# Four layers forward and backward on one core: the last chunks' pieces by a table of their own, a turned weight by TensorE, and another order of the weight gradients

## The chip, the cores and the metric

The kernel runs on one core of a Trainium2 chip, as a single launch. The metric is the device time of that launch in microseconds (us). Engines are named as in the profile: PE is TensorE, DVE is VectorE, ACT is ScalarE, POOL is GpSimd, and SP is the engine whose queue issues the DMAs here.

## The reference

Four residual layers, A, B, A, B, over an input x of 2048 rows and 640 columns (bfloat16); each normalises x, projects to q, k, v (a weight of 640 x 1920), attends with 32 heads of 20 columns, and projects back (640 x 640). A and B use the same weights in both of their layers. What is returned is the output and the gradients for x and for the four weights.

```python
def A(x):            # linear attention
    q, k, v = heads(layernorm(x) @ wqkv_A)
    phi = lambda t: where(t > 0, t + 1, exp(t)) + 1e-6
    pq, pk = phi(q), phi(k)
    kv, z = einsum("bhsd,bhse->bhde", pk, v), einsum("bhsd->bhd", pk)
    num, den = einsum("bhqd,bhde->bhqe", pq, kv), einsum("bhqd,bhd->bhq", pq, z)[..., None] + 1e-6
    return merge(num / den) @ wo_A
def B(x):            # softmax attention over the 256 rows before
    q, k, v = heads(layernorm(x) @ wqkv_B)
    s = where(mask, einsum("bhqd,bhkd->bhqk", q, k) * Dh ** -0.5, -1e9)
    return merge(softmax(s) @ v) @ wo_B
x = x + A(x); x = x + B(x); x = x + A(x); x = x + B(x)
# returned: x, and the gradients of x, wqkv_A, wo_A, wqkv_B, wo_B for a given grad_out
```

## The kernel before

Rows are taken in 16 tiles of 128, and in the backward of B in NC = 8 chunks of two tiles. The layers are numbered 0 (A), 1 (B), 2 (A), 3 (B).

Nearly all of the order is written by hand. A *plan* is a list of (place, function); `slots` sorts it into slots, and a loop runs the functions of each slot, each of which issues a few instructions. So each engine's order is that of the plan. A DMA is issued by SP, in the order in which a scheduler puts the loads and stores; the queue is served in order, so a DMA that waits for its source or its buffer holds up those behind it. Places come from the table `PLACES`.

The stages in order of time:

- **Forward** (to some 650 us). `forward` goes through layers 0 to 3, and a layer's tiles are interleaved with the next's. B1 = 138 is the slot where layer 1 begins its scores. In layer 0 a tile is projected (`dense<-WA,h2T`), mapped by phi (`plan_feat`, pq and pk on DVE) and stored. Beside that the weight of A is turned for later use: `turn(k)` issues 15 transposing DMAs (`tw<-in_A_wqkv_dram`), two every 12 slots from slot 41.6, `keep_turned` stores them, four at a time, to `WTAt` in DRAM; the linear backwards load them back as `WTA`. The turned rows lie in ring buffers of the attention, which `home` gives back.
- **Backward of layer 3** (some 660 to 1099.7). `core` runs the attention backward over the 8 chunks: scores, exponentials, dp, ds, flips of ds, and accumulations (`acc`). In the slots of chunk c there also stand the pieces *behind* an earlier chunk, by `plan_behind` from the table's list `bh`: turn dq (`turn`), dh = dq times the turned weight (`dense<-WTB,dqT`, 30 products a tile), layer norm backward (`ln`, `ln2`: DVE, ACT, POOL's dh and gn), flip gn, multiply by Wo (`dense<-WoTA,gT`, 10 a tile), and from that the linear layer's dn (`prod`, `fold`, `red`), whose outer products with pq (`outer<-dn,pqb`) sum up to dmz. The pieces behind chunk c stand 32 slots after those of c+1's start; for the last chunk 16 earlier than that. What has no slot left in `core` is returned as `left3`.
- **Drain of layer 3** (1099.7 to 1151.7). `left3` runs, with nothing between its pieces but the loads of the next stage; behind its end `close_outer` and `turn_outer` form dmz and dmzT.
- **Linear backward of layer 2** (to some 1263). `plan_linear` for 16 tiles, 8 slots apart: load dn, v, pqk, hn, g, flip them, multiply with mz, dmz, dmzT, then dqkv, dh by `WTA`, layer norm backward. Its first tile begins 3 slots before the drain's end. At its end the first chunk of the next attention backward is prepared (`plan_before`, places `n1`).
- **Backward of layer 1** (to 1692.93) and its **drain** (`left1`, to some 1770), as for layer 3. Between the pieces of this drain stand the first products of the weight gradients.
- **Linear backward of layer 0** (to 1996.8), with weight gradients between: `fill(0.8)` issues 0.8 us of them in each slot.
- **The rest of the weight gradients** (to 2160).

`weight_jobs` yields the weight gradients one product at a time (`wg<-rhs,lhs`). A matrix is made in blocks of 240 or 320 columns (480 for two layers' sum once `W.wide` is set). For each block it loads the right operand (`rhs`), for each matrix the left (`lhs`: hn or o of a layer); in mode `all` both layers are summed, in mode `add` one layer is summed in PSUM and the other's part, made early (`early_weights`, `wgp`) and kept in DRAM, is loaded (`part`) and added. The order of the matrices is

```python
mats = [mat("all", "B", "W", (3, 1)), mat("add", "B", "Wo", (1,)), mat("all", "A", "W", (2, 0)), mat("add", "A", "Wo", (0,))]
```

Of the kernel before, what the change touches and what calls it, by code (L numbers as in the profile page):

```python
# [33 lines left out]
CW = D // 2  # L34
LN_EPS = 1e-5
# [20 lines left out]
class Kern:  # L56
# [183 lines left out]
    def forward(self, st):  # L240
# [59 lines left out]
        def turn(k):  # L300
            i, j = divmod(k, 4)
            if j == 0:
                turned[i] = rings[i].tile([P, 4, D], BF, name=f"tw{i}", tag="T")
            self.dma(turned[i][:, j, :], self.W["A"][:, k * P:(k + 1) * P], transpose=True, behind=True)
# [7 lines left out]
        plan += [(41.6 + 6 * (k // 2), lambda k=k: turn(k)) for k in range(NF)] + [(57.5 + 12 * i, lambda i=i: keep_turned(i)) for i in range(4)] + [(96 + i, lambda i=i: home(i)) for i in range(5)]  # L312
# [605 lines left out]
    def plan_behind(self, st, l, c, dq, g_out):  # L918
# [44 lines left out]
        late = l == 1 and c >= TT // 2 - 2  # L963
        plan = [(0 if ex else 13 if last else A[26], load), (-6 if last else A[27], lambda: turn(0)), (-5 if last else A[28], lambda: turn(1)),
                ((-2 if l == 1 else 14) if last else 26 if l == 3 and c == TT // 2 - 2 else A[29], store), (0 if ex else 13 if late else A[30], load_o), (A[9] + 3, store_g),
                (1 if ex else 14 if late else A[31], load_q), (A[23] + 6, store_dn), (A[24], outer, .54, 0, 378), (A[25], outer, .54, 0, 378)]
        for i in range(2):
            a = A[12 * i:12 * i + 12]
# [649 lines left out]
```

## Time and profile before

| | |
|---|---|
| median of 3 runs | 2164.93 us (2164.41 to 2165.44) |
| the profiled execution | 2161.81 us, its span 2160.1 |
| granted TensorE clock, mean | 0.973 |
| PE busy | 1990.3 us, 92% |
| DVE busy | 1350.9 us, 63% |
| ACT busy | 1362.2 us, 63% |
| POOL busy | 1040.5 us, 48% |
| DMA | 433.48 MB in 729096 packets, 201 GB/s |

The profile is of one execution. Busy times are shares of its span; times in the trace count from the span's start. In a row of the timeline stand the start, the length, the engine, the line, the operation, out<-in by the program's names, shape and type, how many instructions were put together, and in brackets the idle time before and what ended it. A row of several matmuls that follow each other is longer than what they cost, since the last one's way through the array counts: the cost is the distance to the next row's start. In the slices, each digit is a fortieth of the span (54 us) and tells tenths.

### The profile page before, as it was taken

To read this page: it belongs to the slowest core of one execution; us is meant where nothing else is said; L and a number is where in the kernel's file an instruction comes from. 1 tells how busy PE (TensorE), PEld (TensorE's weight loads), DVE (VectorE), ACT (ScalarE), POOL (GpSimd) and SP (SyncE) were. 2 spreads that over 40 slices of the span, in tenths; PEclk is the share of its full clock that TensorE was granted. 3 is DMA by queue.
4 is the path that set the end of the run, shared out by engine and by line. 5 is a ranking of instruction groups with operands and counts; after the bars stand their busy time and mean duration, and the time that the engine had idled before them with its cause. 6 is when DMAs were issued, how large, how long until landed. Compare 5 with 4: busy or idle time off the path is not lost. (4 is left out here: it accounts for less than half of the span.)

```text
span 2160.1 us, 76461 instructions
## 1 busy us (share of the span) xinstructions
PE 1990.3 (92%) x32383; PEld 1547.6 (72%) x32383; DVE 1350.9 (63%) x2765; ACT 1362.2 (63%) x1897; POOL 1040.5 (48%) x1663
## 2 busy tenths in 40 slices
PE   7899998799988999999988989989999889999999
PEld 5567776577766877777767868777777678887546
DVE  6788886878754677777746856777777423333001
ACT  5458888378876788888845767888888414332000
POOL 2046666156666457777643455577776401222000
PEclk9999999999998999999998999999999999999999
DMA  9798897589886779999988962799988987999843
GB/s 275 213 222 218 216 216 170 137 213 220 211 212 189 141 161 189 189 191 180 181 238 266 261 193 75 157 189 189 195 179 182 255 271 229 258 223 249 265 120 93
DMA packets 729096, 433.48 MB, mean 201 GB/s; under 512 B 447024, under 2 KB 711344, under 8 KB 728496
## 3 DMA queue, kind: packets, MB, share of 16 engines
q1 hardware_dynamic: 728752, 428.59, 81.2%
q8 instruction: 253, 4.15, 0.8%
q14 instruction: 91, 0.75, 0.1%
HBM read 194.35 MB, written 144.70 MB: 157 GB/s over the span
## 5 line engine op out<-in xcount | busy, mean ns | idle before, releaser
L763 DVE TENSOR_TENSOR ds<-dp,e 128x1024 bf16<-128x1024 f32 (+1 forms) x384 | 443.7, 1155 | 162.6 <-PE s L146 73.3
L759 ACT ACTIVATE e<-s 128x1024 bf16<-128x1024 f32 (+1 forms) x384 | 378.3, 985 | 89.7 <-PE s L146 84.5
L399 ACT ACTIVATE eT<-sT 128x2048 bf16<-128x2048 f32 x180 | 338.0, 1878 | 96.1 <-PE sT L146 84.8
L146 PE MATMUL wg<-rhs,lhs 128*128 128x240 bf16 (+2 forms) x2400 | 334.0, 294 | 9.7 <-DMA lhs<-hn 9.7
L146 PEld LDWEIGHTS <-lhs 128*128 128x128 bf16 x2400 | 232.6, 99 | 86.1 <-DMA lhs<-hn 12.0
L778 POOL TENSOR_SCALAR_AFFINE_SELECT e<-e 128x256 bf16<-128x256 bf16 x512 | 201.6, 409 | 181.8 <-ACT e L759 150.8
L146 PEld LDWEIGHTS <-dqT 128*128 128x128 bf16 x1920 | 169.8, 98 | 65.8 <-issue 8.7
L407 POOL TENSOR_SCALAR_AFFINE_SELECT eT<-eT 128x512 bf16<-128x512 bf16 x256 | 165.0, 648 | 101.4 <-ACT eT L399 101.4
L792 ACT COPY dsT<-flip 128x1024 bf16<-128x1024 bf16 (+1 forms) x200 | 191.2, 956 | 21.9 <-PE flip L787 20.1
L146 PE MATMUL acc<-slabqs,ds 128*128 128x20 bf16 x2880 | 194.6, 172 | 1.7 <-ACT dq L847 1.0
L146 PE MATMUL acc<-ds,e 128*128 128x20 bf16 x2880 | 192.7, 171 | 0.1
L146 PE MATMUL dp<-slabT,dT 32*128 32x128 bf16 (+1 forms) x1952 | 152.1, 245 | 39.2 <-DVE ds L763 33.7
L146 PEld LDWEIGHTS <-ds 128*128 128x128 bf16 x2880 | 176.2, 96 | 10.6 <-issue 6.6
L774 POOL TENSOR_SCALAR_AFFINE_SELECT e<-e 128x512 bf16<-128x512 bf16 x224 | 142.9, 638 | 62.0 <-ACT e L759 59.0
L146 PEld LDWEIGHTS <-e 128*128 128x128 bf16 x2880 | 164.1, 96 | 7.8 <-issue 2.2
L1148 POOL TENSOR_TENSOR dh<-dh,lg 128x640 f32<-128x640 f32 x32 | 46.0, 1438 | 249.6 <-DVE s L1145 241.4
L146 PE MATMUL dense<-WB,hnT 128*128 128x320 bf16 x960 | 161.3, 302 | 0.5 <-DVE s L522 0.3
L146 PE MATMUL dense<-WTA,dqT 128*128 128x320 bf16 x960 | 161.4, 299 | 0.3 <-DVE dqT L1122 0.3
L146 PE MATMUL dense<-WTB,dqT 128*128 128x320 bf16 x960 | 156.3, 302 | 1.9 <-DMA dqT<-dq 1.9
L146 PE MATMUL s<-slabT,slabqT 32*128 32x128 bf16 (+1 forms) x1952 | 147.6, 245 | 6.6 <-ACT e L759 5.6
L410 POOL TENSOR_SCALAR_AFFINE_SELECT eT<-eT 128x512 bf16<-128x512 bf16 x224 | 143.3, 640 | 18.3 <-ACT eT L399 17.1
L787 PE MATMUL flip<-ident,ds 128*128 128x128 bf16 x1824 | 146.9, 222 | 4.2 <-DVE ds L884 4.0
(180 smaller groups left out, 4220.8 us busy)
## 6 DMA issues: line engine op xcount, KB each, us to landing
T<-T SPq DMA_DIRECT2D x96, 256.0 KB, 3.2
rhs<-dqkv SPq DMA_DIRECT2D x40, 480.0 KB, 5.1
s<-s SPq DMA_DIRECT2D x32, 512.0 KB, 3.8
slabT<-T SPq DMA_DIRECT2D x64, 256.0 KB, 4.0
dqkv<-dq SPq DMA_DIRECT2D x16, 960.0 KB, 5.8
dqkv<-dqa SPq DMA_DIRECT2D x32, 480.0 KB, 4.5
rhs<-dqkv SPq DMA_DIRECT2D x12, 960.0 KB, 7.6
hn<-hn SPq DMA_DIRECT2D x64, 160.0 KB, 2.8
```

Source lines behind the costliest of these rows:

```text
L146: return self.nc.tensor.matmul(out, lhsT=lhsT, rhs=rhs, start=start, stop=stop, skip_group_check=True, **kw)
L399: nc.scalar.activation(e, s, ACT.Exp)
L407: nc.gpsimd.affine_select(out=e, in_=e, compare_op=ALU.is_ge, fill=0.0, base=0, pattern=[[0, 4], [1, P]], channel_multiplier=-1)
L410: nc.gpsimd.affine_select(out=e, in_=e, compare_op=ALU.is_ge, fill=0.0, base=-1, pattern=[[0, 4], [-1, P]], channel_multiplier=1)
L759: nc.scalar.activation(u.e[:, :, 0:w], s[:, :, 0:w], ACT.Exp)
L763: nc.vector.tensor_tensor(out=d.ds[:, :, 0:w], in0=d.dp[:, :, 0:w], in1=d.e[:, :, 0:w], op=ALU.mult)
L774: nc.gpsimd.affine_select(out=v, in_=v, pattern=[[0, 4], [1 if far else -1, P]], **kw)
L778: nc.gpsimd.affine_select(out=v, in_=v, pattern=[[0, 2], [1 if far else -1, P]], **kw)
L787: nc.tensor.transpose(ps[:, 4 * j + i, :], f.ds[:, j, i * P:(i + 1) * P], self.ident)
L792: nc.scalar.copy(v(f.dsT), v(ps))
L1148: nc.gpsimd.tensor_tensor(out=x["dh"], in0=x["dh"], in1=L["g"][:, i, :], op=ALU.add)
```

## The change

It has these parts.

- In the forward, `turn(k)` no longer issues a transposing DMA: five flips on TensorE turn the 640 x 128 block k of A's weight, which is in the SBUF already, and ACT copies the result from PSUM. They stand at slots T0 + T1 k = 108 + 1.5 k; the stores (`keep_turned`) and `home` move behind them.
- The pieces behind the last two chunks of both attention backwards stand by a table of their own, `DRAIN`, counted from slot 32 NC + 7. The last chunk's loads go to buffers of the attention (`gb`, `ob`) and of the tag `dqT`, which has three. The PSUM pool of the drain opens before the first eleven left-over slots (before: behind the first eight). The linear tiles of layer 2 begin at slot 17 of the drain, that is inside it; dmz is closed at 21.2.
- The last tile of layer 2's linear backward has its `ln2` put into the second slot of the next attention; two pools of that attention (pd, pt) are opened at its third visit, since the linear stage's pools close that late. One preparing flip goes from place 9 to 23.
- `weight_jobs`: it starts at the first slot of layer 1's drain, and fills from the sixth; A's W comes ahead of B's Wo; parts are loaded up to 3 (8 at the end) ahead; 8 output buffers in the drain; `FILL` is 0.65 for 0.8; the buffers for the left operands open at other times (the third at slot 48 of the linear stage). `WTA` of layer 0 is loaded behind the first linear tile's loads. In all, 1280 products of 240 columns and 640 of 480 stand for 1600 and 480.

The diff, cut:

```diff
+T0, T1 = 108, 1.5
+DRAIN = {
+    -2: {"load": -3.4, "turn": (0.8, 0.9), "store": (1.3, 6), "o": 0.5, "q": 6, "g": 12, "dn": 16, "outer": (16.2, 16.7),
+         0: [1, 1.1, 1.2, 2, 2.1, 2.2, 2.5, 3.6, 5.6, 7.0, 7.1, 9.5],
+         1: [3.1, 3.2, 3.3, 4, 4.1, 4.2, 4.5, 5.5, 8.5, 9.2, 9.3, 12]},
+    -1: {"load": -2, "turn": (2.9, 3), "store": (3.9, 10), "o": 6.6, "q": 4.6, "g": 16, "dn": 22, "outer": (20.1, 20.5),
+         0: [5, 5.1, 5.2, 6, 6.1, 6.2, 6.5, 8.6, 11, 12.2, 12.3, 16],
+         1: [8, 8.1, 8.2, 9, 9.1, 9.15, 9.45, 10.6, 13, 14.2, 14.3, 20]}}
+FILL = 0.65
...
+        if name == "dqT":
+            bufs = 3
...
-                turned[i] = rings[i].tile([P, 4, D], BF, name=f"tw{i}", tag="T")
-            self.dma(turned[i][:, j, :], self.W["A"][:, k * P:(k + 1) * P], transpose=True, behind=True)
+                turned[i] = rings[4 - i].tile([P, 4, D], BF, name=f"tw{i}", tag="T")
+            tp = st.ps.tile([P, 8, P], BF, name="flip", tag="m")
+            for a in range(DT):
+                nc.tensor.transpose(tp[:, a, :], WA[:, a, k * P:(k + 1) * P], self.ident)
+            nc.scalar.copy(turned[i][:, j, :], tp[:, 0:DT, :].rearrange("p a b -> p (a b)"))
...
-        plan += [(41.6 + 6 * (k // 2), lambda k=k: turn(k)) for k in range(NF)] + [(57.5 + 12 * i, lambda i=i: keep_turned(i)) for i in range(4)] + [(96 + i, lambda i=i: home(i)) for i in range(5)]
+        plan += [(T0 + T1 * k, lambda k=k: turn(k)) for k in range(NF)] + [(T0 + T1 * min(4 * i + 4, NF) + 1, lambda i=i: keep_turned(i)) for i in range(4)]
+        plan += [((B1 - 32 if i == 0 else T0 + T1 * NF + 2), lambda i=i: home(i)) for i in range(5)]
...
-        ex = last and l == 1
-            x["hn"] = self.load(st.ex if ex else st.sp, "hnb", self.pair(self.hn[l], c), [P, 2, D])
-            x["g"] = self.load(st.ex if ex else st.sp, "gc", self.pair(self.gs[l], c), [P, 2, D])
+            x["hn"] = self.load(*((B.sp, "gb") if last else (st.sp, "hnb")), self.pair(self.hn[l], c), [P, 2, D])
+            x["g"] = self.load(*((B.sp, "ob") if last else (st.sp, "gc")), self.pair(self.gs[l], c), [P, 2, D])
...
-            x["o"] = self.load(st.ex if ex else st.sp, "oa", self.pair(self.o[la], c), [P, 2, D])
+            x["o"] = self.load(st.sp, "oa" if not last else "dqT", self.pair(self.o[la], c), [P, 2, D])
...
-            x["pq"] = self.load(st.ex if ex else st.sp, "pqb", self.pair(self.sv[la]["pqk"], c)[:, :, 0:D], [P, 2, D])
+            x["pq"] = self.load(st.sp, "pqb" if not last else "dqT", self.pair(self.sv[la]["pqk"], c)[:, :, 0:D], [P, 2, D])
...
-            a = A[12 * i:12 * i + 12]
+            a = A[12 * i:12 * i + 12] if D0 is None else D0[i]
...
-            plan += [(32 * (c + 2) - (16 if c == NC - 1 else 0) + a, *f)
-                     for a, *f in self.plan_behind(st, l, c, dq, g_out)]
+            at = 32 * NC + 7 if c >= NC - 2 else 32 * (c + 2)
+            plan += [(at + a, *f) for a, *f in self.plan_behind(st, l, c, dq, g_out, B)]
...
+                        if n == 3 and B.late is not None:
+                            B.late()
+                            self.core_buffers2(st, B)
...
-        mats = [mat("all", "B", "W", (3, 1)), mat("add", "B", "Wo", (1,)), mat("all", "A", "W", (2, 0)), mat("add", "A", "Wo", (0,))]
+        mats = [mat("all", "B", "W", (3, 1)), mat("all", "A", "W", (2, 0)), mat("add", "B", "Wo", (1,)), mat("add", "A", "Wo", (0,))]
...
-                if m["mode"] == "add" or nxt[1] is not None and nxt[1]["mode"] == "add" and j > 2:
+                while len(pt) < W.ahead and (m["mode"] == "add" or nxt[1] is not None and nxt[1]["mode"] == "add" and j > 1):
...
-            base = len(left3) - 3
+            base = 17 - 11
...
+                one = self.plan_linear(st, lp, 2, t, X, WTA, self.gs[1])
+                if t == TT - 1:
+                    ln2 = one.pop(-3)[1]
...
-            hooks = self.slots([(a - 20, f) for a, f, *_ in fs if a >= 20], 8)
+            hooks = self.slots([(2, ln2)] + [(a - 20, f) for a, f, *_ in fs if a >= 20], 8)
...
-                if j == 8:
+                if j == 0:
                     next(jobs)
-                if j == 20:
-                    self.dma(WTA.rearrange("p a b -> p (a b)"), self.WTA)
-                if j > 24:
+                if j > 4:
                     fill(1.0)
...
-                    fill(0.8)
-            W.lhs += [wl, wl3]
+                    if n == 8:
+                        self.after(self.dma(WTA.rearrange("p a b -> p (a b)"), self.WTA), lp.loaded)
+                    if n == 48:
+                        W.lhs += [wl3]
+                    fill(FILL)
+            wl4 = self.pool(rest, "wl", 1)
+            W.lhs += [wl4, wl, wl]
```

More of the change, by code (lines that the diff above doesn't have):

```diff
@@ L962, in plan_behind @@
         A = PLACES["bh"]
[L963 to L966, printed above, removed]
+        D0 = DRAIN.get(c - TT // 2)
+        if D0 is not None:
+            plan = [(D0["load"], load), (D0["turn"][0], lambda: turn(0)), (D0["turn"][1], lambda: turn(1)), (D0["store"][l // 2], store), (D0["o"], load_o),
+                    (D0["g"], store_g), (D0["q"], load_q), (D0["dn"], store_dn), (D0["outer"][0], outer), (D0["outer"][1], outer)]
+        else:
+            plan = [(A[26], load), (A[27], lambda: turn(0)), (A[28], lambda: turn(1)), (A[29], store), (A[30], load_o), (A[9] + 3, store_g),
+                    (A[31], load_q), (A[23] + 6, store_dn), (A[24], outer), (A[25], outer)]
         for i in range(2):
-            a = A[12 * i:12 * i + 12]
+            a = A[12 * i:12 * i + 12] if D0 is None else D0[i]
             t = 2 * c + i
@@ L1209, in part @@
         def part(m, c0, j, w):
-            t = W.out.tile([P, 320], F32, name="pt", bufs=3)
+            t = W.pts.tile([P, 320], F32, name="pt", bufs=W.ahead)
             self.dma(t, m["part"][:, j * D + c0:j * D + c0 + w])
@@ L1473, in passes @@
             for t in range(TT):
-                plan += [(max(base + 8 * t + a, 0), f) for a, f in self.plan_linear(st, lp, 2, t, X, WTA, self.gs[1])]
+                one = self.plan_linear(st, lp, 2, t, X, WTA, self.gs[1])
+                if t == TT - 1:
+                    ln2 = one.pop(-3)[1]
+                plan += [(max(base + 8 * t + a, 0), f) for a, f in one]
             def begin():
@@ L1533, in passes @@
             self.turn_outer(st, self.dmz, self.dmzT)
+            W.out = out
             psl.close()
@@ L1548, in passes @@
                     plan += [(8 * t + a + 14, f) for a, f in self.plan_linear(st, lp, 0, t, X, WTA, self.out_gx)]
-                for f in self.slots(plan, int(max(a for a, *_ in plan)) + 1):
+                for n, f in enumerate(self.slots(plan, int(max(a for a, *_ in plan)) + 1)):
                     if f is not None:
                         f()
-                    fill(0.8)
-            W.lhs += [wl, wl3]
+                    if n == 8:
[5 more added lines that the diff above has]
+            W.lhs += [wl4, wl, wl]
             W.wide, W.wq2 = True, self.pool(rest, "wq2", 1)
-            W.out, W.most = self.pool(rest, "wo2", 4), 480
+            W.out, W.most, W.ahead = self.pool(rest, "wo2", 4), 480, 8
+            W.pts = W.out
             fill(1e9)
```

47 lines of the change are left out of this document (26 added, 21 removed).

## The prediction

> **What bounds the kernel now.** I read the page's head and engine shares first, then its slices, then busy time by stretch, and last the timeline of TensorE in each stretch where it is idle.
>
> ```profile
> span 2160.1 us, 76461 instructions
> PE 1990.3 (92%) x32383; PEld 1547.6 (72%) x32383; DVE 1350.9 (63%) x2765; ACT 1362.2 (63%) x1897; POOL 1040.5 (48%) x1663
> ...
> PE   7899998799988999999988989989999889999999
> ...
> PEclk9999999999998999999998999999999999999999
> ```
>
> TensorE is busy for 92% of the span: the kernel is bound by it, and what can be won by moving work is the 169.8 us in which it is idle, and the places where its clock is below 1. Of the places that the digits show, the change touches the start (7, 8), the 21st and 22nd slice (from 1080) and the 32nd and 33rd (from 1674); a share over a slice hides a short wait, so the rows by stretch give their size (columns: length, busy time of PE, PEld, DVE, ACT, POOL with counts, then granted clock, DMA share, GB/s):
>
> ```profile
> 95.00:121.48 26.48, 20.28 (x158) 13.88 (x157) 20.64 (x57) 3.78 (x7) 1.10 (x2) 0.81 0.39 113
> 1099.70:1151.66 51.96, 37.95 (x298) 27.41 (x295) 17.85 (x42) 16.90 (x33) 20.09 (x16) 0.83 0.87 286
> 1200.00:1240.00 40.00, 39.97 (x480) 32.96 (x478) 34.10 (x68) 29.82 (x61) 17.87 (x13) 1.00 1.02 264
> 1692.93:1776.00 83.07, 69.79 (x614) 57.47 (x611) 19.27 (x45) 17.30 (x36) 20.11 (x16) 0.91 0.97 300
> 1840.00:1880.00 40.00, 40.00 (x428) 35.66 (x426) 13.66 (x34) 13.56 (x28) 8.27 (x6) 1.00 1.03 250
> 1996.80:2010.00 13.20, 6.89 (x34) 4.60 (x34) 0.41 (x1) 0.00 (x0) 0.00 (x0) 0.65 1.04 341
> ```
>
> The two drains (the left-over pieces behind the attention backward of layer 3, from 1099.70, and of layer 1, from 1692.93) leave TensorE idle for 14.0 and 13.3 us; behind the last linear tile, at 1996.8, 6.3 of 13.2 us are idle at clock 0.65. Inside the linear backwards (1200 to 1240, 1840 to 1880) nothing is idle. The change touches all of these places; the attention backwards themselves keep their order, so I cost the places one by one and take the rest as it is.
>
> **Part 1, forward: A's W turned by TensorE.** The forward's first layer, in its steady state, has a period that the flips of hn show:
>
> ```profile
> 49.13 0.44 PE L163 MATMUL flip<-ident,hn 128*128 128x128 bf16 x5
> ...
> 53.82 0.44 PE L163 MATMUL flip<-ident,hn 128*128 128x128 bf16 x5
> ...
> 58.73 2.83 PE L146 MATMUL dense<-WA,h2T 128*128 128x320 bf16 x10 [3.78 <-DVE pk L602]
> ...
> 64.01 0.44 PE L163 MATMUL flip<-ident,hn 128*128 128x128 bf16 x5
> ...
> 78.48 0.44 PE L163 MATMUL flip<-ident,hn 128*128 128x128 bf16 x5
> ...
> 84.87 0.33 PE L163 MATMUL flip<-ident,hn 128*128 128x128 bf16 x3
> ```
>
> ```profile
> 58.18 0.49 DVE L602 SCALAR_TENSOR_TENSOR pk<-dense,e 128x320 bf16<-128x320 f32 x1 [4.13 <-DMA pqk<-pk]
> ```
>
> ```profile
> 49.19 3.51 SPq L110 DMA_TRANSPOSE tw<-in_A_wqkv_dram  x2
> ...
> 53.43 0.38 SPq L110 DMA_DIRECT2D pqk<-pk  x1
> ```
>
> The period is 53.82 - 49.13 = 4.69 us, so 53.82 to 64.01 loses 10.19 - 4.69 = 5.5 and 78.48 to 84.87 loses 6.39 - 4.69 = 1.7: 7.2 us. TensorE waits for DVE's pk, DVE for the store of an earlier pk to leave its buffer, and that store sits in SP's queue behind two transposes that hold the queue for 3.51. The change takes all 15 transposes out of that queue, and I see nothing else there that comes late: 7.2 goes. In their place stand 15 groups of five flips on TensorE. Five take 49.41 - 49.13, about 0.28 us of the engine (the next dense starts there), 4.2 in all. Some six fall into its busy stretch and cost 6 x 0.28 = 1.7. The other nine fall behind 95 us, where it has 26.48 - 20.28 = 6.2 idle, waiting for DVE, at clock 0.81: at most 9 x 0.28 / 0.81 = 3.1, and I take half, 1.5. The 15 copies of 128x640 go to ACT, busy for 3.78 of 26.48 there, so nothing. Gain 7.2 - 3.2 = **4.0** (0.5, if half the stall has another cause and the rest is paid in full, to 7.2, if the flips cost nothing).
>
> The row shows a clock of 0.81 in that stretch, and I credit the flips with nothing for it. [...]
>
> **Part 2, drain of layer 3.** TensorE and POOL:
>
> ```profile
> 1105.83 8.31 PE L146 MATMUL dense<-WTB,dqT 128*128 128x320 bf16 x60
> 1115.35 0.45 PE L163 MATMUL flip<-ident,gn 128*128 128x128 bf16 x5 [1.21 <-POOL gn L1009]
> 1117.93 1.52 PE L146 MATMUL dense<-WoTA,gT 128*128 128x320 bf16 x5 [2.13 <-ACT gT L166]
> ...
> 1123.64 0.84 PE L146 MATMUL dense<-WoTA,gT 128*128 128x320 bf16 x5
> ...
> 1131.45 0.84 PE L146 MATMUL dense<-WTB,dqT 128*128 128x320 bf16 x5
> ...
> 1144.96 0.86 PE L146 MATMUL outer<-dn,pqb 128*120 128x126 bf16 x6 [3.84 <-DVE dn L1034]
> ...
> 1149.78 1.03 PE L210 MATMUL flip<-ident,dmz 120*126 120x120 bf16 x6 [1.11 <-DVE dmz L203]
> ...
> 1151.66 0.69 PE L146 MATMUL dense<-dmzT,vT 126*128 126x120 bf16 x7 [0.58 <-ACT dmzT L211]
> ```
>
> ```profile
> 1111.66 1.40 POOL L1002 TENSOR_TENSOR dh<-dh,gc 128x640 f32<-128x640 f32 x1 [15.40 <-DVE s L999]
> 1113.76 1.53 POOL L1009 TENSOR_TENSOR gn<-dh,lna 128x640 bf16<-128x640 f32 x1 [0.69 <-POOL dh L1002]
> ```
>
> The last of the 120 WTB products (dh of the last tile) ends at 1131.45 + 0.84 = 1132.29, 32.6 us into the drain; from there one chain (layer norm on DVE, dh and gn on POOL, flip, gT, WoTA, dn, outer, dmz turned) ends 19.4 later at 1151.66, where the first linear tile goes on. The new table puts ahead of that last product only the 45 flips of dq, the 120 WTB, 10 WoTA, 10 flips of gn and 12 outers: 130 x 8.31 / 60 = 18.0, 67 x 0.28 / 5 = 3.8, one wait for a copy, together 22. The chain behind it is the same 19.4, so 41.5 for 51.96: 10.4. I take **10** (6 to 14). Upwards: the first linear tile's flips and loads now stand inside the chain's idle time. Downwards: POOL now does four dh and four gn, with the products' folds among them, and if the last gn comes behind one more dh, gn and fold (1.40 + 1.53 + about as much), 4 are lost. Two loads of the last chunk now take buffers of the tag "dqT", so SP waits for a product to release one, and behind it wait the stores of dq and the first linear tile's loads; since three such buffers turn over every 15 products (2 us), I put that inside the 4.
>
> **Part 3, the join of the linear backward of layer 2 to the attention of layer 1.**
>
> ```profile
> 1272.81 0.69 DVE L763 TENSOR_TENSOR ds<-dp,e 128x512 bf16<-128x512 f32 x1 [8.19 <-DMA g<-lgn]
> ```
>
> ```profile
> 1268.60 1.54 POOL L1155 TENSOR_TENSOR lgn<-dh,lna 128x640 bf16<-128x640 f32 x1
> ```
>
> ```profile
> 1265.54 0.99 ACT L913 COPY dT<-flip 128x1024 bf16<-128x1024 bf16 x1
> ```
>
> DVE stands still for 8.19 here, and the attention's first pieces wait with it. The last tile's lgn (POOL, until 1270.14) stands ahead of the masks of the first scores, and a turn of dT (ACT, 0.99) ahead of their exponentials. The change puts the first two slots into the attention, the other 14 places later, and it opens two pools of the attention (pd, pt) only after three slots. I take **2.5**, the 1.54 and the 0.99; 0 if the pools opened late give the wait back, 4 at most, about half the 8.19.
>
> **Part 4, drain of layer 1, with weight gradients between.**
>
> ```profile
> 1731.31 0.78 PE L146 MATMUL wg<-rhs,lhs 128*128 128x240 bf16 x3 [1.09 <-DMA lhs<-hn]
> ...
> 1750.15 4.26 PE L146 MATMUL wg<-rhs,lhs 128*128 128x240 bf16 x40
> ...
> 1770.90 0.90 PE L163 MATMUL flip<-ident,ldn 128*126 128x128 bf16 x6 [4.37 <-DMA ldn<-dn]
> ```
>
> ```profile
> 1758.90 2.64 SPq L110 DMA_DIRECT2D lhs<-o  x4
> ```
>
> Idle are 13.3, shared among waits of some 1 us for the weight products' lhs (as at 1731.31) and those of the chain; 4.37 of it is the first linear tile's load behind four loads for Wo's products in SP's queue (2.64); Wo comes third now, so these are gone from there. The weight jobs load at the drain's first step and not at its ninth, and fill from its sixth. Of the idle time I leave 8: 5 in the chain before the first weight products have their operands, 2 at ldn, and 1 since WTA is loaded behind that tile. Gain 13.3 - 8 = 5.3, I take **5** (0 to 8); the clock's loss, 69.79 x 0.09 = 6.3, I leave as it is.
>
> **Part 5, linear backward of layer 0, and its end.**
>
> ```profile
> 2001.26 0.98 PE L146 MATMUL wg<-rhs,lhs 128*128 128x240 bf16 x4 [4.43 <-DMA lhs<-hn]
> ```
>
> Behind the last linear tile TensorE waits for the operands of A's W: 6.31 idle and 6.89 x 0.35 = 2.4 for the clock. With fill 0.65 some 200 products of B's W are left at that point, 200 x 4.26 / 40 = 21 us, under which A's operands come in (the new buffer opens there; four loads with 2.64 of issue land well inside 21). Gain **8.7** (4.5 if the last of them lands late, to 9). In the stage itself:
>
> ```profile
> 1225.78 0.51 PE L163 MATMUL flip<-ident,ldn 128*126 128x128 bf16 x6
> 1232.36 0.51 PE L163 MATMUL flip<-ident,ldn 128*126 128x128 bf16 x6
> ```
>
> A linear tile alone takes 6.58 at DMA share 1.02, which is 6.7 us of DMA. Between its parts stand now 51 weight products a tile (5.3 us, 12 in all), at 1.03, so 12.3 of DMA, 5.6 of it theirs. With 0.65 / 0.8 of them a tile is 6.58 + 4.3 = 10.9, and its DMA 6.7 + 4.6 = 11.3: share 1.04, where the trace has shown 1.03 without idle time. I take a loss of **0.5** (0, to 6 if 1.00 is a ceiling: 0.4 x 16). The products left out here come later at the same price: 160 of 480 columns for 320 of 240, nothing.
>
> **The sum**: 4.0 + 10 + 2.5 + 5 + 8.7 - 0.5 = 29.7. The profiled execution took 2161.81 (its span and 1.7 around it), so 2132.1; the median of the runs is 3.1 above it, so **2135**. All low ends (0.5 + 6 + 0 + 0 + 4.5 - 6 = 5) give 2160, all high ones (42.2) 2123.
>
> **Rivals.** *The drains stay chains.* POOL and the one-chunk chain hold both drains, which give 3 and 2 where I have 10 and 5: 2145. For it: the 19.4 of the chain are untouched; against: 120 products move ahead of it, and 5.3 us of waits in between. *The operands at the end come late after all*, 6 of 8.7 stay: 2141. Both: 2151. *The linear stage of layer 0 becomes bound by DMA.* With thinner filling each tile's transposed loads come late, and TensorE waits at every tile. It needs 29.7 / 16 = 1.9 us a tile to decide; at 3 it costs 48, and the time is 2183, slower than before. For it: a DMA share of 1.03; against: layer 2's tiles run at 1.02 with 39.97 of 40 busy and no filling. *Full clock in the drains.* Waits of 1.21 and 2.13, with a flip between, are followed by a group at 1.52 where a later one takes 0.84. If the shorter waits that stay (2 us or less) no longer drop the clock, 7 more come back (6.3 in one drain, a little of the other): 2128. [...] *The change does nothing of note*: the waits move on unchanged, 2165.
>
> **How the numbers follow.** My forecast 0.52 (its own range 2124 to 2141), late operands or chained drains 0.28, both 0.07, full clock 0.05, nothing 0.02, slower 0.06. The range, 2119 to 2154, takes in the first rivals and all but the last of the low ends. A measurement of this kernel tells 0.2% (4.3 us) from no change; every case but two is faster by more: 0.92, 0.02, 0.06.
>
> **What would show it.** Right: no wait over 1 us for pk around 58 us, and a first layer shorter by 4; the drain of layer 3 at 41 to 42 us with a last WTB product 22 into it; no wait for lhs over 1 us at the end of the linear stage; linear tiles of layer 0 at 10.9 with TensorE never idle. Wrong: the last gn of POOL over 3 us behind its DVE step, a wait for ldn as before, or a tile of 12 or more. A result over 2154 would mean that a linear tile waits for DMA.

## The result, and the profile after

The changed kernel takes 2132.2 us (median of 4 runs, 2121.9 to 2139.9) against 2164.7 for the kernel before; the ratio is 0.984 with a 95% interval of 0.982 to 0.987. The forecast was 2135, in a range of 2119 to 2154. The profiled execution took 2129.71, its span 2128.0, which is 32.1 less than before. The head, the shares and the slices of the changed kernel's page:

```profile
span 2128.0 us, 76279 instructions
PE 1980.1 (93%) x32298; PEld 1529.8 (72%) x32298; DVE 1350.8 (63%) x2762; ACT 1367.7 (64%) x1910; POOL 1038.9 (49%) x1663
...
PE   7989999899988999999998989999998989999999
...
PEclk9999999999989999999999999999999999999999
```

TensorE was idle for 169.8 us and is for 147.9: 21.9 of the 32.1 are waits that went. The other 10.2 are less busy time, although 75 flips (4.2 us) came on top: the same work ran at a higher clock (0.980 in the mean for 0.973). The trace's records of the granted clock, which is at half rate for stretches of 3.41 us and multiples of it, have 116.1 us at half rate before the last product of the kernel before and 85.3 of the changed one; half of the difference is 15. A part of that can be chance: over the traces of the runs below it is 58 to 102 in the ten others with the new drains, and 82 and 137 in the two others with the old ones.

The same marks in both timelines give this ledger (us; the last stretch goes to the span's end):

| stretch | before | changed | gain | forecast |
|---|---|---|---|---|
| to layer 1's first score product | 121.48 | 114.10 | 7.4 | 4.0 |
| to layer 1's first product with WoB | 16.18 | 18.57 | -2.4 | - |
| to the drain of layer 3 | 962.04 | 963.22 | -1.2 | 0 |
| that drain, to the first product with dmzT | 51.96 | 44.94 | 7.0 | 10 |
| layer 2's linear backward | 111.91 | 110.54 | 1.4 | 0 |
| join, to the first early weight product | 10.31 | 8.00 | 2.3 | 2.5 |
| attention of layer 1 | 419.05 | 418.42 | 0.6 | 0 |
| drain of layer 1, linear stage, weight gradients | 467.17 | 450.21 | 17.0 | 13.2 |
| sum | 2160.1 | 2128.0 | 32.1 | 29.7 |

The stretches in the changed kernel, in the columns of the prediction's rows by stretch:

```profile
87.60:114.10 26.50, 20.82 (x223) 15.72 (x222) 21.57 (x60) 11.88 (x21) 1.10 (x2) 1.00 0.65 209
114.10:132.67 18.57, 15.12 (x213) 10.93 (x214) 13.09 (x37) 8.78 (x6) 7.85 (x14) 0.91 1.10 255
1095.89:1140.83 44.94, 35.61 (x298) 26.53 (x295) 17.20 (x42) 16.59 (x33) 20.44 (x16) 0.84 0.84 290
1251.37:1259.37 8.00, 4.57 (x52) 2.55 (x53) 1.88 (x5) 5.83 (x10) 7.67 (x11) 0.84 0.76 199
1677.79:1732.59 54.80, 45.56 (x423) 36.47 (x419) 16.29 (x39) 15.79 (x33) 20.45 (x16) 0.96 0.94 285
1732.59:1930.37 197.78, 197.78 (x2093) 174.49 (x2093) 71.16 (x179) 77.84 (x160) 45.25 (x30) 0.99 1.00 262
1930.37:2124.14 193.77, 193.77 (x1164) 113.70 (x1162) 19.82 (x38) 7.08 (x14) 2.94 (x2) 1.00 0.58 181
```

and, between the same marks, in the kernel before:

```profile
121.48:137.66 16.18, 13.89 (x213) 10.33 (x214) 13.32 (x38) 8.78 (x6) 8.07 (x14) 1.00 1.07 273
1263.57:1273.88 10.31, 4.87 (x44) 2.77 (x44) 2.03 (x5) 5.81 (x8) 8.01 (x12) 0.66 0.75 195
1692.93:1770.90 77.97, 64.69 (x581) 53.11 (x577) 18.07 (x42) 16.95 (x35) 20.11 (x16) 0.94 0.97 300
1990.13:2156.67 166.54, 160.23 (x994) 98.62 (x992) 14.88 (x30) 6.33 (x13) 2.94 (x2) 0.97 0.53 160
```

The drain of layer 1 has 9.2 us idle for 13.3, and from the end of the linear stage to the last product TensorE is never idle, where it was for 6.3. The drain of layer 3 in TensorE's timeline of the changed kernel, with the first flip, the last WTB products, the waits behind them, and the chain's end; then the first linear tile's load of layer 0:

```profile
1095.89 1.76 PE L1068 MATMUL flip<-ident,dq 128*128 128x128 bf16 x15
...
1119.20 2.20 PE L157 MATMUL dense<-WTB,dqT 128*128 128x320 bf16 x15
...
1125.74 1.58 PE L157 MATMUL dense<-WoTA,gT 128*128 128x320 bf16 x10 [2.41 <-ACT gT L177]
1129.07 0.71 PE L174 MATMUL flip<-ident,gn 128*128 128x128 bf16 x5 [1.74 <-POOL gn L1026]
...
1140.83 0.69 PE L157 MATMUL dense<-dmzT,vT 126*128 126x120 bf16 x7 [0.85 <-ACT dmzT L222]
...
1732.59 0.90 PE L174 MATMUL flip<-ident,ldn 128*126 128x128 bf16 x6 [3.72 <-DMA ldn<-dn]
```

The last product with WTB now starts 25.2 us into the drain (32.3 before), and from it to the first product with dmzT it takes 19.7 us, as before. The drain's first flips, at 1.76 for 15, run at half rate here.

### The profile page after: what moved, and what is told of

Same layout as the page of the kernel before. It is cut to its first block, busy times and chain, and to the rows that moved or that the text cites. A ratio compares the mean times of both kernels' runs of the same rounds, so it can differ in the third digit from the quotient of the medians.

```text
span 2128.0 us, 76279 instructions
## 1 busy us (share of the span) xinstructions
PE 1980.1 (93%) x32298; PEld 1529.8 (72%) x32298; DVE 1350.8 (63%) x2762; ACT 1367.7 (64%) x1910; POOL 1038.9 (49%) x1663
## 5 line engine op out<-in xcount | busy, mean ns | idle before, releaser
L157 PE MATMUL wg<-rhs,lhs 128*128 128x240 bf16 (+2 forms) x2240 | 327.0, 300 | 1.0 <-DMA lhs<-hn 1.0
L157 PEld LDWEIGHTS <-lhs 128*128 128x128 bf16 x2240 | 215.3, 98 | 89.5 <-DMA lhs<-hn 1.2
L157 PEld LDWEIGHTS <-dqT 128*128 128x128 bf16 (+1 forms) x1944 | 170.5, 98 | 65.3 <-issue 9.7
L425 POOL TENSOR_SCALAR_AFFINE_SELECT eT<-eT 128x512 bf16<-128x512 bf16 x224 | 142.4, 636 | 19.2 <-ACT eT L414 18.7
```

The costliest lines, as they stand in the source:

```text
L157: return self.nc.tensor.matmul(out, lhsT=lhsT, rhs=rhs, start=start, stop=stop, skip_group_check=True, **kw)
L425: nc.gpsimd.affine_select(out=e, in_=e, compare_op=ALU.is_ge, fill=0.0, base=-1, pattern=[[0, 4], [-1, P]], channel_multiplier=1)
```

## The experiments

Times of single executions of one kernel lie 3 to 21 us apart, and half-rate stretches come and go in parts that no kernel here touches (from the first WoB product to layer 3's drain, for one, it takes 955 to 971 us in 14 traces, with 20 to 55 us of it at half rate). So a part's effect is read from the time between marks in the trace, and the ratio to the kernel before stands beside it.

**The forward part alone**, in the kernel before:

```diff
-            self.dma(turned[i][:, j, :], self.W["A"][:, k * P:(k + 1) * P], transpose=True, behind=True)
+            (five flips and a copy, as in the change, at slots 108 + 1.5 k; the stores and home moved)
```

> The kernel before with only the forward part: A's W turned by 15 groups of five flips on TensorE at slots 108 and up, no transposing DMAs of it. Theory (the part stands on its own): the waits for pk at 58, 70, 79 and 81 us are gone, the first score product of layer 1 (sT, 121.5 us before, 114.1 after) comes at 114, and layer 1's first product with WoB (137.7 before, 132.7 after) at 132 to 133; the whole is 4 to 6 us shorter. Rival (the gain of the forward is a clock that happened to be high in the one run looked at): first score product at 117 to 119.

The first score product comes at 113.75, the first WoB product at 132.23 (137.66 before), and the ratio is 0.9977 (0.9959 to 0.9996): 5 us, with an interval of 1 to 9. The part stands on its own, at what the changed kernel shows. The waits for pk are gone in it. Of the 7.7 us, 2.3 are given back in the stretch behind, where DMA's share is over 1 in both kernels of the pair (1.07 and 1.10). How much comes back varies: that stretch takes 15.9 to 20.5 us, at the median 18.5, in the twelve traces without the transposing DMAs, and 16.2 and 17.6 in the two with them.

**The flips taken out** of the changed kernel:

```diff
-            for a in range(DT):
-                nc.tensor.transpose(tp[:, a, :], WA[:, a, k * P:(k + 1) * P], self.ident)
-            nc.scalar.copy(turned[i][:, j, :], tp[:, 0:DT, :].rearrange("p a b -> p (a b)"))
+            nc.scalar.copy(turned[i][:, j, :], WA[:, 0, 0:D])
```

> The changed kernel without the 75 flips on TensorE: ACT copies untransposed columns of A's weight, so the gradients that use it are left wrong; all else stays. Theory (flips count for the clock): without them the granted clock of 88 to 114 us falls from 1.00 to below 0.9 and the first score product comes at 113.5 to 116, no earlier than the 114.1 with them. Rival (flips only cost their time, 4.2 us of TensorE, and the gaps are too short to lose the clock): clock 1.00 without them, first score product at 110 to 112.5.

**The flips added** to the kernel before, the transposing DMAs kept:

```diff
+        def idle(k):
+            tp = st.ps.tile([P, 8, P], BF, name="flip", tag="m")
+            for a in range(DT):
+                nc.tensor.transpose(tp[:, a, :], WA[:, a, k * P:(k + 1) * P], self.ident)
+        plan += [(108 + 1.5 * k, lambda k=k: idle(k)) for k in range(NF)]
```

> The kernel before, with the 75 flips added at slots 108 and up into a PSUM tile that nobody reads; the transposing DMAs stay. Theory (flips count for the clock): the granted clock of the stretch from 95 us to the first score product rises from 0.81 to 0.95 or more, and that product comes at 119 to 121.5 in spite of 4.2 us more work. Rival (they do not count): clock 0.81 as before, that product at 122.5 to 125.

The stretch ahead of the first score product, first without the flips (to be held against the changed kernel's 87.60:114.10), then with the flips added (against the prediction's 95.00:121.48):

```profile
87.60:114.34 26.74, 20.27 (x162) 13.50 (x161) 21.14 (x59) 11.00 (x20) 1.09 (x2) 0.87 0.61 202
```

```profile
95.00:121.43 26.43, 20.76 (x222) 15.72 (x221) 21.55 (x60) 4.36 (x9) 1.09 (x2) 1.00 0.41 118
```

Without the flips the clock falls from 1.00 to 0.87 (two stretches at half rate) and the product comes at 114.34, not earlier than the 114.10 with them. With the flips added, the clock rises from 0.81 to 1.00 and the product comes at 121.43 for 121.48, with 64 matmuls more in the row. So in both pairs the clock of this stretch is the higher one with the flips in it (1.00 for 0.87, 1.00 for 0.81), as the theory has it. That this is why they cost nothing does not follow. In the changed kernel, and then without the flips:

```profile
101.22 0.34 PE L174 MATMUL flip<-ident,o 128*128 128x128 bf16 x3 [1.61 <-DVE o L506]
```

```profile
101.30 0.34 PE L174 MATMUL flip<-ident,o 128*128 128x128 bf16 x3 [1.95 <-DVE o L503]
```

Nine of the row's eleven groups of flips stand ahead of this wait for DVE, which ends at the same time with and without them: they lie in TensorE's idle time, whatever the clock. Behind it come 12.9 us with two groups at full rate and 13.0 without any, 3.4 of them at half rate; here the clock may have paid for the flips. No run holds the clock fixed, so the two reasons are not told apart. The whole time does not move in either (0.9854 against the change's 0.9843; 1.0007, 0.9986 to 1.0027).

**The linear tiles behind the drain**, not inside it:

```diff
-            base = 17 - 11
+            base = 22 - 11
```

> The changed kernel with layer 2's linear tiles beginning five slots later, behind the drain's last outer product and not inside the drain. Theory (the drain's length is 25 us to the last WTB product and then the chain of 19.4): the time from the drain's first flip to the first product with dmzT stays at 45, and what is lost is the flips of the first tile behind the chain, about 2 us; the whole 1 to 3 us longer. Rival (the gain of this drain comes from the tiles standing inside it): 5 us or more longer.

From the drain's first flip to the first product with dmzT it takes 42.1 us here, of which 22.2 to the last WTB product (I had expected 45, from the changed kernel's one profiled execution); layer 2's linear backward is as long as in the changed kernel (110.4). The whole is at 0.9853 (0.9836 to 0.9870), not told apart from the change. So the tiles inside the drain are worth 2 us at most, and the drain's gain is left to the table, with the buffers that go with it; no run takes the table alone back. It also shows what the changed kernel's profiled execution hid: without half rate at the drain's start, the last WTB product comes at 22.2, in this kernel and in all others with the table. Over the seven kernels that leave this drain as the change has it, the drain takes 40.4 to 44.9, at the median 41.4, against 51.9 to 52.0 in the three that have the old one.

**More filling in layer 0's linear stage**, then **less**:

```diff
-FILL = 0.65
+FILL = 0.72
```

> The changed kernel with 0.72 us of weight products in each slot of layer 0's linear stage for 0.65: some 70 products more in the stage, so 130 of B's W (13 us) and not 200 (21 us) are left behind the last linear tile. Theory (what was won at the end is cover for the loads of A's left operands): those land late again, TensorE waits 4 to 8 us for lhs behind the last tile and its clock may drop, so the time from the drain's last WTB product of layer 1 to the end is 5 to 10 us longer than the 424 of the changed kernel. Rival (the operands come early enough anyway): that time stays within 2 us.

```diff
-FILL = 0.65
+FILL = 0.5
```

> The changed kernel with 0.5 us of weight products in each slot of layer 0's linear stage for 0.65: a tile of 9.9 us on TensorE, with 10.2 of DMA at the shares seen (6.7 for the tile, 3.5 for the products). Theory (DMA is no ceiling here, as it was not at a share of 1.00): TensorE stays busy through the stage, and the time from the drain's last WTB product of layer 1 to the end stays within 2 us of 424. Rival (DMA becomes the bound once the filling is thin, the mechanism by which the change could have been slower): TensorE waits in every tile for dqT or ldn, 4 us or more longer.

Layer 0's linear stage with 0.5, and the group of the stage's products with WTA (idle time before them at the end):

```profile
1724.09:1907.72 183.63, 177.22 (x1878) 153.84 (x1879) 70.00 (x175) 76.25 (x157) 45.26 (x30) 0.98 0.98 261
```

```profile
L157 PE MATMUL dense<-WTA,dqT 128*128 128x320 bf16 x479 | 81.0, 301 | 5.1 <-DMA dqT<-dqa 5.1
```

With 0.72, the time from the last WTB product of layer 1 to the end is 424.1, as in the changed kernel, and TensorE is busy for all of the 183.0 behind the linear stage: the theory I gave for this run fell. The cover left was less than I had reckoned: 93 products of B's W, by the trace, some 9.5 us, where the changed kernel has 202 (21 us). The last load of A's left operands lands 10.2 us behind the stage's last product with WTA here, and 2.5 behind it in the changed kernel, so that 0.72 comes near to a wait. With 0.5 the time is 432.2, 8.0 more (the whole at 0.9876, 0.9854 to 0.9899): in the linear stage TensorE is idle for 6.4 of 183.6, of which 5.1 are waits for dqT to be turned by DMA, whose share in the stage is 0.98, and 1.1 a wait for a load. The waits stand in four of the sixteen tiles, 3.79 us in one place, and not in every tile as the rival of the prediction that makes the kernel slower had it. Its mechanism is there, in one trace and at a part of its price; at 0.65, with 197.78 busy of 197.78, it has not begun.

**The left operands of A's W both asked for behind the linear stage**:

```diff
-                    if n == 48:
-                        W.lhs += [wl3]
...
-            W.lhs += [wl4, wl, wl]
+            W.lhs += [wl3, wl4, wl, wl]
```

> The changed kernel with both left operands of A's W (hn of layers 2 and 0) loaded behind the last linear tile; in the changed kernel one of them gets its buffer at slot 48, inside the stage. Theory (the 200 products left of B's W, 21 us, cover both loads, as the prediction's step has it): no wait for lhs over 1 us, the time from the last WTB product of layer 1 to the end stays within 1.5 us of 424. Rival (the wait is gone because one operand is loaded long before): a wait of 2 us or more for lhs behind B's W and 3 to 8 us more in all.

```profile
1935.74:2129.51 193.77, 193.77 (x1164) 113.70 (x1162) 19.83 (x38) 7.08 (x14) 2.94 (x2) 1.00 0.58 181
```

Behind the linear stage nothing waits. But this does not test the cover for both loads, since the edit did not move the first: the scheduler of the DMAs puts the first operand's four loads inside the stage as before, as SP's timeline of this run shows (the first three of them):

```profile
1787.50 0.52 SPq L119 DMA_DIRECT2D lhs<-hn  x1
...
1792.62 2.09 SPq L119 DMA_DIRECT2D lhs<-hn  x2
```

In the changed kernel they stand at 1777.5 to 1785.6, and in both kernels only the second operand comes at the end (there it is issued from 1922.5 to 1926.6 and lands by 1932.9, 2.5 us behind the stage's last product). So the 21 us cover four loads, with much to spare; eight are untested. The time to the end is 427.6, over the limit that I set, but the 3.5 lie in the drain ahead (36.2 for 32.6), where the two kernels issue the same DMAs in the same order; what made them there is open.

**The old order of the matrices**:

```diff
-        mats = [..., mat("all", "A", "W", (2, 0)), mat("add", "B", "Wo", (1,)), ...]
+        mats = [..., mat("add", "B", "Wo", (1,)), mat("all", "A", "W", (2, 0)), ...]
```

> The changed kernel with the old order of the matrices (B's W, B's Wo, A's W, A's Wo). Theory (the order matters only for the loads that stand in SP's queue before the first linear tile): the four loads of o come back ahead of ldn's load in the drain of layer 1, and the wait there grows from 3.7 by 1 to 3 us; at the end of the linear stage nothing changes, since 21 us of products of B's W cover o and g as well; the whole 0 to 4 us longer. Rival (the order is what removed the wait at the end): a wait of 3 us or more for lhs behind the linear stage, 6 us or more longer.

```profile
1963.12 1.65 PE L157 MATMUL wg<-rhs,lhs 128*128 128x320 bf16 x8 [2.40 <-DMA rhs<-g]
```

The time to the end is 427.4, 3.3 more, within the theory's 0 to 4, but not where it has them: the wait for ldn in the drain is 3.95 for 3.72, and 2.7 are a wait for Wo's right operand behind the linear stage. No lhs is waited for there, so the order is not what took the 6.3 us of waits at the end away. Nor did it take Wo's loads from ahead of ldn's: with the old order too the first loads of o are issued at 1776.7, long behind ldn's at 1727.6.

**The join as before**:

```diff
-                if t == TT - 1:
-                    ln2 = one.pop(-3)[1]
...
-            fs = self.plan_before(st, 1, 0, B, ((*PLACES["n1"][1:5], 23), PLACES["n1"][6:11]), -10, True)
+            fs = self.plan_before(st, 1, 0, B, (PLACES["n1"][1:6], PLACES["n1"][6:11]), -10, True)
```

> The changed kernel with the join of layer 2's linear backward to layer 1's attention as before: the last tile's ln2 in its own place, the preparing flip at place 9; the two pools still open late. Theory (these two moves are what made the join shorter): from the first score product of the join to the first early weight product 10 us again (10.3 before, 8.0 changed), the whole 2 us longer. Rival (the join got shorter by the pools opened late, or by the clock of that one run): 8 to 8.5 us as changed.

```profile
1252.19:1262.11 9.92, 4.80 (x47) 2.70 (x45) 1.88 (x5) 6.09 (x10) 8.33 (x12) 0.70 0.71 187
```

9.9 us for the 8.0. With the new join it takes 7.5 to 8.6 in ten traces, with the old 10.2 to 10.4 in three, so the two moves are worth 1.3 to 2.4, and the pools opened late 0.5 at most. The clock is not the reason: with 5.6 us at half rate the new join takes 8.2 (the run with the late tiles), the old one here, with 6.0, 9.9. The whole (0.9861, 0.9835 to 0.9887) can't show it.

**A fold moved on POOL**, in both drains:

```diff
-                     (a[10], lambda f=prod: f(1), .49, 0, 1600), (a[10], fold), (a[11], red, .45, 0)]
+                     (a[10], lambda f=prod: f(1), .49, 0, 1600),
+                     (10.7 if D0 is not None and i and not last else a[10], fold), (a[11], red, .45, 0)]
```

> The changed kernel with one step of both drains moved: the folds of the second tile of the last chunk but one (two POOL operations, 2.1 us) go from ahead of the last tile's dh on POOL to behind its gn. Theory (POOL's order sets the end of the chain: the last tile's dh starts at 1126.00, right behind a fold, though its layer norm step on DVE was done at 1124.15): the last gn comes 1.5 to 2 us earlier, and the time from the last WTB product to the first product with dmzT falls from 19.2 to 19.7 by 1 to 2, in the drain of layer 1 likewise up to its last outer product. Rival (the fold moved is itself on the chain, by the outer products that need it): unchanged or up to 1 us longer.

POOL's last dh and gn in the changed kernel, then with the fold moved:

```profile
1126.00 1.40 POOL L1019 TENSOR_TENSOR dh<-dh,ob 128x640 f32<-128x640 f32 x1
1127.48 1.53 POOL L1026 TENSOR_TENSOR gn<-dh,part 128x640 bf16<-128x640 f32 x1
```

```profile
1121.87 1.40 POOL L1019 TENSOR_TENSOR dh<-dh,ob 128x640 f32<-128x640 f32 x1 [1.29 <-DVE s L1016]
1123.35 1.54 POOL L1026 TENSOR_TENSOR gn<-dh,part 128x640 bf16<-128x640 f32 x1
```

Counted from the start of the last WTB product (1121.10 and 1118.87) the gn starts at 4.5 instead of 6.4, 1.9 earlier, and the dh ahead of it now waits for DVE. This is POOL's order: the gn starts at 6.4 in all nine traces with the change's folds, and at 4.5 in both with the fold moved. What arrives at the end isn't shown. The last fold, now behind the one that was moved, ends at 13.8 (15.2 in the changed kernel, but 13.6 to 15.2 over those nine), and the first product with dmzT comes at 18.9 (19.7, but 18.2 to 20.9). The ratio, 0.983 (0.980 to 0.985), is the lowest of all, and not told apart from the change's.

**Flips of the identity in the drains' waits**, first in the flip's own PSUM tile, then in tiles of their own together with the moved fold:

```diff
+        self.warm(warm[0], t)        # 20 ahead of the last tile's flips of gn
...
+        self.warm(warm[1], t)        # 24 and 8 behind the copies of the last chunk's gT
```

> The changed kernel with flips of the identity into unread parts of PSUM, 24, 20 and 8 of them (1.3, 1.1 and 0.4 us), put into the three longest waits of TensorE in both drains' chains (2.4, 1.7 and 0.8 us). Theory (flips count for the clock, as in the forward): the half-rate windows behind the last WTB product, 3.4 to 12 us long in the runs so far, are 3.4 or less, and the time from that product to the first with dmzT is 18 to 19 us (18.3 to 20.9 so far). Rival (they do not, or what is at half rate there waits for POOL anyway): 19.2 to 20.7, with half-rate windows as before.

```diff
+                if last and k == 0:
+                    self.warm((40, 12)[i], st.ps.tile([P, 8, P], BF, name="warm", tag="m"))
...
+            plan += [(21.15 - 11, lambda: self.warm(24, st.ps.tile([P, 8, P], BF, name="warm", tag="m")))]
```

> The changed kernel with the folds moved behind the last gn in both drains, and with flips of the identity in PSUM buffers of their own, so that they do not wait for ACT: 40 and 12 ahead of the last chunk's two WoTA groups, and 24 ahead of dmz's flips in the drain of layer 2. Theory (flips count for the clock, and POOL's order costs a little): from the last WTB product to the first product with dmzT 17.5 to 18.5 us, with half-rate windows of 3.4 or less behind it up to the join; the whole 1 to 4 us shorter than the changed kernel. Rival (the chain waits for DVE, ACT and POOL, whose time no clock of TensorE moves): 18.9 or more, the whole as the changed kernel.

In the first, the 24 and the 8 flips waited for ACT's copy (2.41 and 0.83) and so filled nothing; the drain takes 41.5, with 6.8 us at half rate from 1137.3 on. The 19.25 from the last WTB product to dmzT are the rival's number, and so is the half rate, but with two of three waits unfilled the run tests little (the whole at 0.9855, 0.9818 to 0.9892). In the second they fill the two waits (0.18 is left of 2.41, 0.17 of 0.84):

```profile
1129.15 2.40 PE L185 MATMUL warm<-ident 128*128 128x128 bf16 x40
...
1139.47 0.35 PE L157 MATMUL outer<-dn,dqT 128*120 128x126 bf16 x3 [0.52 <-DVE dn L1053]
1141.50 1.10 PE L157 MATMUL outer<-dn,dqT 128*120 128x126 bf16 x9 [1.67 <-DVE dn L1053]
...
1142.70 2.73 PE L185 MATMUL warm<-ident 128*128 128x128 bf16 x24
```

Half rate does not come where the flips stand, but at 1140.6, among the short products with waits of 0.52, 0.52 and 1.67 where I had put none, and lasts for 10.2. From the last WTB product to dmzT it is 19.8, the whole at 0.987 (0.985 to 0.989). These are the rival's numbers. But it does not follow that TensorE's clock has no part in the chain, since the flips did not take the half rate away. Over the seven kernels that leave this drain as it is, the time from the last WTB product to dmzT goes with the time at half rate in it: 18.2 us with 0.7 at half rate, 18.3 to 19.2 with 3.4, 19.7 with 6.9, 20.7 and 20.9 with 12.4 and 12.2. The last ten products with WoTA, whose results the chain needs, take 2.85 in the changed kernel (at 1130.62), at half rate, and 1.53 in the run with the left operands asked for late:

```profile
1127.61 1.53 PE L157 MATMUL dense<-WoTA,gT 128*128 128x320 bf16 x10 [0.84 <-ACT gT L177]
```

So the waits for DVE, ACT and POOL make most of the chain, and the clock goes with up to 2.7 us of it.

## Why the prediction was right, and where it was not

**The sum** was 29.7, the profiled executions are 32.1 apart. That the two lie so close is in part luck, with terms off to both sides (+1.0, -3.0 and +3.8 in the ledger) and executions of one kernel up to 21 us apart. Right by its steps: the drain of layer 3 in its length (22 to the last WTB product, then 19.4: measured 22.2 and 18.2 to 20.9, 41.4 at the median for 41.5; the 7.0 of the ledger is the execution with half rate at its start), the join (2.5; measured 1.3 to 2.4), and the waits at the end, 6.3 and gone. The idle time of layer 1's drain is right only in the two profiled executions (5; 13.3 - 9.2 = 4.1): over the traces it is 9.2 to 12.4 with the change's drain (without the runs that fill it with flips) and 10.9 to 13.3 with the old one, some 2 us apart at the medians. Which part of the change took the waits at the end away is open: the old order alone and a filling of 0.72 alone do not bring them back, and the run that asked for both loads late did not get the first one late. The tiles of layer 0:

```profile
1855.19 0.54 PE L174 MATMUL flip<-ident,ldn 128*126 128x128 bf16 x6
...
1866.57 0.54 PE L174 MATMUL flip<-ident,ldn 128*126 128x128 bf16 x6
```

11.38 where I had 10.9, in the nine last of fifteen (12.2 in two, 10.9 in one), with no idle time; the 0.5 that I took off for DMA was not due. The tile before had 64 weight products and 12.6 us, not 51 and 12; now it has 52. So DMA had 0.5 us a tile more room than I gave it, and the share is 1.00, not 1.04.

**The chain of layer 3's drain is as long as before, but not the same.** The prediction named as a loss of up to 4 that POOL's last gn comes behind one more dh, gn and fold, and as a sign of being wrong that this gn starts over 3 us behind its DVE step. Both came. The DVE step of the last tile in the changed kernel, and its gn on POOL:

```profile
1123.94 0.21 DVE L1018 TENSOR_SCALAR s<-ac 128x1 f32<-128x1 f32 x1
```

```profile
1127.48 1.53 POOL L1026 TENSOR_TENSOR gn<-dh,part 128x640 bf16<-128x640 f32 x1
```

That is 3.3 us behind, and 6.4 behind the last WTB product's start where it was 3.4. From the gn to dmzT it then takes 13.4 where it took 16.3, so that 3.0 lost and 3.0 won cancel. What is shorter, by the timelines: in the kernel before, the first linear tile's flips hold back the last outer product, which starts at 1147.81 although its dn was ready at 1144.82; now they stand in a wait for DVE. The prediction named this gain too, without a size. That the two cancel, and the chain kept its 19.4, is luck. Another sign of being wrong, a wait for ldn as before, came as well (below).

**The forward step failed in its clock term.** The 7.2 of waits went as said; but the flips, priced at 3.2 and credited with no clock, cost nothing: most stand in a wait for DVE, and the clock rises from 0.81 to 1.00. No run shows that flips leave the clock where it is, as the sum had it; the runs with the flips taken out (0.87 for 1.00) and added (1.00 for 0.81) show the opposite, in this stretch. That 2.4 come back in the stretch behind I had not seen: by the two rows it is idle for 1.2 more, waiting for loads of T, and busy for 1.2 more at a clock of 0.91. So 7.4 - 2.4 = 5.0 is near the 4.0 by two errors of opposite sign.

**The clock was the mis-sized term** of parts 4 and 5. I counted 2.4 for it at the end and left drain 1 as it was. From that drain's first flip to the last product the kernel before has 24.4 us at half rate, the changed one 10.2; half of 14.2 is 7.1. With 4.1 + 6.3 of waits that makes 17.5, measured 17.0, forecast 13.2. This one holds beyond the pair: 20 to 28 us at half rate in the three traces with the old drain, 4 to 10 in the eleven with the new.

**The wait for ldn** (2 left in the sum) stayed at 3.72. Wo's loads are gone from ahead of it (not by their order, as the run with the old one shows), but the queue stands behind three stores of weight products that are not made yet, as SP's timeline of the changed kernel shows:

```profile
1722.28 5.19 SPq L119 DMA_DIRECT2D out_dram<-wr  x3
1727.57 0.38 SPq L119 DMA_DIRECT2D rhs<-dqkv  x1
1728.04 0.53 SPq L119 DMA_DIRECT2D ldn<-dn  x1
```

**The rivals.** The drains did not stay chains of the old length, and the operands did not come late. The linear stage that waits for DMA is real with a filling of 0.5 (6.4 us idle, 8 in the time to the end) and absent at 0.65. Full clock in the drains did not come: a wait of 2.41 is followed by half rate at 1127.1 in the changed kernel.

## What to carry to other kernels

Where a chain of several engines follows the last of many products, put those products first: the drain got shorter by about as much as its last product came earlier (41.4 us for 51.9, with that product at 22.2 for 32.3), and what filled the chain's gaps was worth 2 us at most. An edit that asks for a load later moves it only if the scheduler follows: look for its issue in the queue's timeline before reading the time. A load's wait is found by reading what stands ahead of it in the queue, and a store of a result that is not yet made stands there as long as that result takes: three such stores held the queue for 5.19 us here, and the last of their results was copied by ACT at 1726.75, 4.5 us behind the start of the three. A kernel whose busy engine shifts between two rates from execution to execution, as TensorE does here between 1.00 and 0.50, is measured part by part between marks in the trace; a part of 2 us is not seen in the whole.

## What the runs showed of the hardware

In the records of the pair's two traces the granted clock of TensorE is 1.00 or 0.50 and nothing between, and up to the last product each stretch at 0.50 is 3.41 us long or two, three or four times that: 20 stretches in the kernel before (116.1 us in all), 15 in the changed one (85.3).

The length of a single wait does not tell where they come. In the changed kernel the half rate sets in at 1127.1, behind a wait of 2.41 us that ends at 1125.74, at 1140.7, behind one of 1.48 that ends at 1139.14, and at 1731.3, inside the 3.72 of the wait for ldn. But the forward's row from 87.60 to 114.10 has a wait of 1.61 and keeps a clock of 1.00; without the flips the same place has a wait of 1.95, and the row a clock of 0.87. With flips of the identity in two of the chain's waits, the half rate came at 1140.6 all the same, among waits of 0.52, 0.52 and 1.67.

What was tested by an edit is the flips of the forward. With the 75 flips the clock of the stretch ahead of the first score product was 1.00 in the changed kernel and in the kernel before with the flips added; without them it was 0.87 and 0.81. No run tells what else the half rate depends on.
